# Two PSUM banks reduced by one VectorE instruction in an attention kernel, with a new order of the banks

## The chip, the cores and the metric

The kernel runs on one core of a Trainium2 chip. A core has a matrix engine (TensorE, PE in the profile, with its weight loads shown apart as PEld), a vector engine (VectorE, DVE), a scalar engine (ScalarE, ACT), GpSimd (POOL) and a queue engine that here only issues transfers (SyncE, SP). They run side by side and wait for one another through semaphores. TensorE writes its results to PSUM, a memory of eight banks; one bank holds 128 rows of 512 fp32 numbers. The metric is the time of one execution on the device, in microseconds; lower is better. An execution with the profiler on gives the trace.

## The reference

The function mixes two causal or full attention layers over the same `x` (2,048 rows of 512), each with 32 heads of 16 dimensions:

```python
x = A_x
g = _sigmoid((x * gate_w).sum(-1, keepdims=True))
a = _A_ref(x, A_wqkv, A_wo)
b = _B_ref(x, B_wq, B_wk, B_wv, B_wo, B_beta)
return g * a + (1 - g) * b
```

`_A_ref` is plain softmax attention of every row over all 2,048 rows:

```python
scores = jnp.einsum("bhqd,bhkd->bhqk", q, k) * scale
p = _softmax(scores, axis=-1)
o = jnp.einsum("bhqk,bhkd->bhqd", p, v)
```

`_B_ref` cuts the rows into 4 segments of 512. Within a segment it is causal softmax attention; a memory matrix carried from segment to segment adds a second part, and a gate by head mixes the two. A softmax subtracts the maximum of each row of scores, and it is these row maxima that the change is about.

## The kernel before

**Units, slots, bursts.** The attention is cut into units `(side, g, c)`: side A or B, a group `g` of four heads, and a block `c` of 512 query rows. There are 32 units of each side. A unit of side A has 64 slots, one for each 128 keys and each head; a unit of side B, which is causal and local, has 10. That makes 2,368 slots (`nS`), which the main loop (L1001 and after) walks in order `n`. In each slot `score_part(n)` issues the score product of 128 keys by 512 queries into one of three `st` banks (L726), and ScalarE turns it into exponentials (L749). After every third slot, a burst (`BURST = 3`), TensorE also gets the products of older exponentials with the values, into the one bank `ops` (L783). How many pieces of 128 columns it takes is set by `most()`, so bursts differ. Instead of value products a burst can hold three products of an output projection (L895) or of a later projection (L666).

**Maxima.** Scores are built with keys as rows, so the maximum of a query's scores must be known before its unit starts. It comes from a second set of products with queries as rows: `max_part(m, bank)` issues, for slot `m = n + LEAD` (96 slots ahead), one product of 128 queries by 512 keys (`max_product`, L205) into a PSUM bank, and VectorE reduces that bank to one maximum for each row (L226). For side B, where the mask matters, a slot holds one or two products of different widths in one bank, and VectorE takes each one's maximum under the causal mask by `tensor_tensor_reduce` (L238 in the profile, a custom instruction and a read of its accumulator). The first of the two is issued at once; the second waits in `rows_left` until after the next reduction. When a unit's last maximum is in, `finish_max` combines them (L183), GpSimd splits the result, TensorE transposes it and a transfer puts it into two rows of the unit's queries, so that the score product subtracts the maximum by itself. The list `maxs` fixes which slot has which maximum; those of side B fall on slots with `m % 3 == 0`, the first of a burst.

**The order on TensorE.** It is the order in which the program is written: score, maximum, score, maximum, score, maximum, then the value products of the burst. A score and the maximum product beside it use different halves of the array's rows. TensorE takes its instructions in this order, and one that waits holds those behind it.

**Banks.** Of the eight PSUM banks three are `st`, one is `ops`, and four are the banks of the maxima, made at L606 as four tiles:

```python
banks = [sm_ps.tile([128, CH], F32, name=f"sm{i}") for i in range(4)]
...
max_part(m, lambda: banks[m % 4])
```

So slot `m` uses bank `m % 4`, and its product waits until the reduction of slot `m - 4` is done. The 96 maxima ahead of the main loop (`some_max`) use other tiles, `me_sm`, in the prologue. In the last 96 slots (`wide`), which have no maxima left, the banks serve as further score banks, and at the end they collect the last output products (`close`).

**Waits.** The semaphores are set by the recording layer: it knows which tile an instruction reads or writes and adds a wait where two instructions of different engines touch the same tile.

Of the kernel before, what the change touches and what calls it, by code (L numbers as in the profile page):

```python
# [22 lines left out]
CH = 512  # L23
# [4 lines left out]
SCALE = 0.25  # L28
# [19 lines left out]
def gated_mix(ctx, tc, x, xT, wqkv, a_wo, b_wq, b_wk, b_wv, b_wo, beta, gate_w, out):  # L48
    nc = tc.nc
# [85 lines left out]
    qt, kt_ = {}, {}  # L135
# [33 lines left out]
    def rows(t, h, n):  # L169

        return t[64 * (h // 2):64 * (h // 2) + n, h % 2]
# [19 lines left out]
    def transpose_max(us, pool, tag):  # L191
# [8 lines left out]
        for i, (_, u, ms) in enumerate(us):  # L200
            for r in range(2):
                nc.sync.dma_start(raw(qt[u])[64 * r + 48:64 * r + 50], raw(mt)[32 * i + 16 * r:32 * i + 16 * r + 16])

    def max_product(ps, u, h, s, n0, n, k, k0=0):
        nc.tensor.matmul(ps[:, n0:n0 + n], rows(qt[u][:, :, s * 128:(s + 1) * 128], h, 48), rows(k[:, :, k0:k0 + n], h, 48),  # L205
                         start=True, stop=True)

    rows_left = []

    def flush_rows():  # L210
        while rows_left:
            rows_left.pop(0)()

    def max_part(m, bank):

        u, (r, i) = maxs[m]
        side, g, c = u
        if u not in pmt:
            pmt[u] = mp.tile([128, 4, 4] + [4] * (side == "A"), F32, tag="pm" + side, name="pm")
        pm = pmt[u]  # L220
        ps = bank()
        if side == "A":

            kc, s, h = i // 8, i % 8 // 2, 2 * r + i % 2
            max_product(ps, u, h, s, 0, CH, kt_[u, kc])
            nc.vector.tensor_reduce(pm[:, h, s, kc:kc + 1], ps, axis=AX.X, op=ALU.max)  # L226
            flush_rows()
        else:


            k = kt_[u, c]
            mine = [(2 * r + h, s, 128 * (s == 2) + 256 * (s == 1 and h), 128 * (s + 1))
                    for h, s in (((0, 0), (0, 2)), ((0, 1), (1, 1)), ((1, 0), (1, 2)), ((0, 3),), ((1, 3),))[i]]
            for h, s, n0, w in mine:
                max_product(ps, u, h, s, n0, w, k)
            flush_rows()
            for h, s, n0, w in mine:
                rows_left.append(lambda h=h, s=s, n0=n0, w=w: nc.vector.tensor_tensor_reduce(  # L238
                    out=tri["rest"][:, 0:w], in0=ps[:, n0:n0 + w], in1=tri["mask"][:, CH - w:], scale=-1.0, scalar=3.0e38,
                    op0=ALU.add, op1=ALU.min, accum_out=pm[:, h, s:s + 1]))  # L240
# [464 lines left out]
    def from_bank(n):  # L705

        return nc.vector.tensor_copy if n > wide.start + 4 else nc.scalar.copy
# [3 lines left out]
    def score_part(n):  # L711

        u, j = slots[n]
        side, g, c = u
        q = qt[u]

        if j % 4 == 0:
            pt_[u, j // 4] = pp.tile([128, 4, CH], F32, tag="p", name="p")
            order_p[u, j // 4] = len(order_p)
            assert not queue or order_p[queue[0][1], queue[0][2] // 4] > len(order_p) - 1 - NP  # L720
        p = pt_[u, j // 4]
        h = (0, 2, 1, 3)[j % 4]

        def score(ps, h, b, k, n0, q0):

            nc.tensor.matmul(ps[:, n0:n0 + CH - q0], rows(k[:, :, b * 128:(b + 1) * 128], h, 50),  # L726
                             rows(q[:, :, q0:], h, 50), start=True, stop=True)

        def diagonal(x):
            nc.gpsimd.affine_select(out=x, in_=x, pattern=[[0, 4], [1, 128]], base=0, channel_multiplier=-1,  # L730
                                    compare_op=ALU.is_ge, fill=0.0)

        ps = banks[1 + n % BURST] if n in wide and n // BURST % 2 else st_ps.tile([128, CH], F32, tag="st", name="st")
        if side == "A":
            score(ps, h, j // 4 % 4, kt_[u, j // 16], 0, 0)
        else:
            k = kt_[u, c]
            if j < 8:
                score(ps, h, j // 4, k, 0, 128 * (j // 4))
                if j >= 4:  # L740
                    score(ps, h, 3, k, 384, 384)
            else:
                for f in range(2):
                    score(ps, 2 * (j - 8) + f, 2, k, 256 * f, 256)
        if side == "B" and j >= 8:
            nc.scalar.activation(p[:, 2 * (j - 8):2 * (j - 8) + 2, 0:256], ps.rearrange("p (h t) -> p h t", h=2), AF.Exp,
                                 scale=SCALE)
        else:
            nc.scalar.activation(p[:, h], ps, AF.Exp, scale=SCALE)  # L749
# [141 lines left out]
    def products(ps, t, b, side, o, start, stop):  # L891

        assert (side, o) in ready
        for i, (x, w) in enumerate(((1, 0), (0, 1), (0, 0))):
            yield lambda i=i, x=x, w=w: nc.tensor.matmul(ps, t[:, b, x], halved[side][:, o, w], start=start and i == 0,  # L895
                                                         stop=stop and i == 2)

    def out_rows(c, b):
        return out[c * CH + b * 128:c * CH + (b + 1) * 128, :]
# [31 lines left out]
    part = {}  # L931

    def keep(ps, c, b):
        part[b] = fr.tile([128, D], F32, tag="part", name="part")
        nc.scalar.copy(part[b], ps)

    def leave(ps, c, b):
        t = fr.tile([128, D], F32, tag="res", name="res", bufs=2)
        from_bank(n)(t, ps)
# [97 lines left out]
    for b in range(4):  # L1037
        close(0, "A", NO - 1, b)
        for _, f in fill[-3:]:
            f()  # L1040
        t = fr.tile([128, D], F32, tag="v" if b % 2 else "res", name="res", bufs=2)
        if b < 3:
            (nc.vector.tensor_copy if b % 2 else nc.scalar.copy)(t, banks[b])
            nc.sync.dma_start(out_rows(last, b), t)
            continue

        for cols, copy, queue in ((slice(0, 256), nc.scalar.copy, nc.scalar), (slice(256, 512), nc.vector.tensor_copy, nc.sync)):
            copy(t[:, cols], banks[b][:, cols])
            queue.dma_start(out_rows(last, b)[:, cols], t[:, cols])


# [33 lines left out]
```

## Time and profile before

| | us |
|---|---|
| median of three runs | 1785.6 (1783.46 to 1789.0) |
| the profiled execution, its own time | 1784.4 |
| its span, first to last instruction | 1782.7 |
| maximum reductions (L226), mean of one | 0.682 |
| exponentials (L749), mean of one | 0.601 |
| score products (L726, side A), mean of one | 0.432 |
| maximum products (L205, side A), mean of one | 0.428 |

The profile has views of one execution: busy time by engine; the chain of work that ended last, followed back from the last instruction; groups of equal instructions with their line, operation, tiles and shapes, their count, busy time, mean time, and the idle time of the engine ahead of them with what ended it; a list of waits; a timeline; and sums over stretches of the span. Times are in us unless ns stands beside them. `x1916` is a count. The mean of one instruction runs from its start to its end and can be longer than the spacing of two that follow each other, since they overlap; the ends of TensorE's products are modelled. The granted clock of TensorE was 1.00 of full speed over the whole main loop.

### The profile page before, as it was taken

To read this page: it belongs to the slowest core of one execution; us is meant where nothing else is said; L and a number is where in the kernel's file an instruction comes from. 1 tells how busy PE (TensorE), PEld (TensorE's weight loads), DVE (VectorE), ACT (ScalarE), POOL (GpSimd) and SP (SyncE) were. 2 spreads that over 40 slices of the span, in tenths; PEclk is the share of its full clock that TensorE was granted. 3 is DMA by queue.
4 is the path that set the end of the run, shared out by engine and by line. 5 is a ranking of instruction groups with operands and counts; after the bars stand their busy time and mean duration, and the time that the engine had idled before them with its cause. 6 is when DMAs were issued, how large, how long until landed. Compare 5 with 4: busy or idle time off the path is not lost.

```text
span 1782.7 us, 40694 instructions
## 1 busy us (share of the span) xinstructions
PE 1773.5 (99%) x14945; PEld 912.4 (51%) x14945; DVE 1574.0 (88%) x3330; ACT 1437.9 (81%) x2754; POOL 640.9 (36%) x748
## 2 busy tenths in 40 slices
PE   9999999999999999999999999999999999999999
PEld 7887776444444444444444444444444444444444
DVE  4235777999999999999999999999999999999930
ACT  5455444888888888888888888888888888888884
POOL 3002222414161416443434343343434253435343
PEclk9999999999999999999999999999999999999999
DMA  7667555445463436544454544454545353544542
GB/s 227 219 226 249 189 195 192 132 103 140 108 169 107 134 116 180 147 136 135 134 134 128 146 127 146 128 146 115 157 106 156 115 142 116 147 119 140 144 161 61
DMA packets 142422, 261.55 MB, mean 147 GB/s; under 512 B 36328, under 2 KB 60680, under 8 KB 141712
## 3 DMA queue, kind: packets, MB, share of 16 engines
q1 hardware_dynamic: 140864, 257.69, 49.6%
q8 instruction: 119, 1.95, 0.5%
q0 software_dynamic: 1216, 1.14, 0.2%
q14 instruction: 79, 0.65, 0.1%
q10 hardware_dynamic: 144, 0.13, 0.0%
HBM read 174.39 MB, written 83.25 MB: 145 GB/s over the span
## 4 chain that ended last, share of the span: by engine, by line
PE 93%; DMA 2%; ACT 2%; DVE 1%; POOL 1%; issue 0%; SPq 0%; POOLq 0%; DVEq 0%; ACTq 0%
PE ops L783 33%; PE st L726 27%; PE sm L205 14%; PE pr L314 9%; PE ops L895 4%; PE ops L666 2%; PE sm L895 2%; DMA raw<-xT 1%; POOL mn L374 1%; PE num L496 1%; DMA qdA<-q 0%; DMA vs<-wqkv 0%; DMA qdB<-q 0%; DVE q L377 0%; ACT full L369 0%
## 5 line engine op out<-in xcount | busy, mean ns | idle before, releaser
L749 ACT ACTIVATE p<-st 128x512 f32<-128x512 f32 x2261 | 1189.4, 601 | 152.5 <-PE sm L205 108.6
L226 DVE TENSOR_REDUCE pm<-sm 128x1 f32<-128x512 f32 x2048 | 1280.8, 682 | 11.8 <-PE sm L205 11.6
L726 PE MATMUL st<-qA,kA 50*128 50x512 f32 x2014 | 663.1, 432 | 0.0
L205 PE MATMUL sm<-kA,qA 48*128 48x512 f32 x2048 | 658.9, 428 | 0.2
L783 PE MATMUL ops<-p,vA 128*17 128x128 f32 (+3 forms) x6432 | 551.9, 442 | 0.0
L726 PEld LDWEIGHTS st<-qA,kA 50*128 50x128 f32 x2014 | 327.5, 185 | 415.6 <-ACT p L749 371.0
L205 PEld LDWEIGHTS sm<-kA,qA 48*128 48x128 f32 x2048 | 330.6, 185 | 15.2 <-issue 6.4
L845 POOL TENSOR_TENSOR rcp<-rec,minus 128x32 f32<-128x32 f32 x43 | 234.2, 5446 | 76.3 <-DMA rec<-dend 71.7
L238 DVE CUSTOM_DVE_ANT_0 rest<-sm,mask 128x128 f32<-128x128 f32 (+3 forms) x512 | 247.3, 483 | 1.8 <-PE sm L205 0.3
L783 PEld LDWEIGHTS ops<-p,vA 128*17 128x17 f32 x6432 | 130.4, 96 | 214.7 <-issue 189.7
L730 POOL TENSOR_SCALAR_AFFINE_SELECT p<-p 128x512 f32<-128x512 f32 x128 | 79.4, 637 | 332.4 <-ACT p L749 327.9
L205 PE MATMUL sm<-kB,qB 48*128 48x128 f32 (+3 forms) x512 | 166.2, 384 | 0.0
L726 PE MATMUL st<-qB,kB 50*128 50x512 f32 (+1 forms) x495 | 109.4, 329 | 0.3 <-ACT mt L199 0.3
L377 DVE TENSOR_TENSOR q<-full,q 128x512 fp32r<-128x512 f32 x56 | 38.9, 694 | 70.2 <-ACT q L370 69.3
L726 PEld LDWEIGHTS st<-qB,kB 50*128 50x128 f32 x495 | 69.9, 186 | 59.3 <-ACT p L749 48.7
L783 PE MATMUL ops<-p,vB 128*17 128x128 f32 (+3 forms) x1504 | 87.5, 350 | 0.0
L205 PEld LDWEIGHTS sm<-kB,qB 48*128 48x128 f32 x512 | 79.9, 184 | 0.0
L187 POOL CAST ms<-nm 128x16 fp32r<-128x16 f32 x32 | 6.7, 208 | 203.1 <-DVE nm L183 201.3
L374 POOL TENSOR_SCALAR mn<-full 128x512 f32<-128x512 f32 x24 | 35.7, 1488 | 102.1 <-ACT full L369 81.7
L369 ACT COPY full<-pr 128x512 f32<-128x512 f32 x56 | 32.6, 582 | 39.3 <-PE pr L314 39.0
L187 POOL CAST ms<-pm 128x16 fp32r<-128x16 f32 x32 | 6.3, 196 | 128.5 <-DVE pm L238 128.4
L861 POOL TENSOR_TENSOR v<-v,inv 128x512 f32<-128x512 f32 x31 | 39.9, 1286 | 25.8 <-DMA inv<-rdA 22.1
(190 smaller groups left out, 1626.1 us busy)
## 6 DMA issues: line engine op xcount, KB each, us to landing
kA<-kdA SPq DMA_DIRECT2D x256, 128.0 KB
vA<-vdA SPq DMA_DIRECT2D x31, 544.0 KB
kA<-kdA SPq DMA_DIRECT2D x256, 64.0 KB
kdA<-q SPq DMA_DIRECT2D x32, 256.0 KB
qdB<-q SPq DMA_DIRECT2D x32, 256.0 KB
qA<-qdA SPq DMA_DIRECT2D x64, 128.0 KB
kdB<-q SPq DMA_DIRECT2D x32, 256.0 KB
qB<-qdB SPq DMA_DIRECT2D x64, 128.0 KB
```

The costliest lines, as they stand in the source:

```text
L205: nc.tensor.matmul(ps[:, n0:n0 + n], rows(qt[u][:, :, s * 128:(s + 1) * 128], h, 48), rows(k[:, :, k0:k0 + n], h, 48), start=True, stop=True)
L226: nc.vector.tensor_reduce(pm[:, h, s, kc:kc + 1], ps, axis=AX.X, op=ALU.max)
L238: rows_left.append(lambda h=h, s=s, n0=n0, w=w: nc.vector.tensor_tensor_reduce(out=tri["rest"][:, 0:w], in0=ps[:, n0:n0 + w], in1=tri["mas ...
L314: nc.tensor.matmul(ps, l(a, k), r(b, k), start=(n == 0), stop=(n == 11))
L374: nc.gpsimd.tensor_scalar_min(ph["mn"], full, 0.0)
L726: nc.tensor.matmul(ps[:, n0:n0 + CH - q0], rows(k[:, :, b * 128:(b + 1) * 128], h, 50), rows(q[:, :, q0:], h, 50), start=True, stop=True)
L730: nc.gpsimd.affine_select(out=x, in_=x, pattern=[[0, 4], [1, 128]], base=0, channel_multiplier=-1, compare_op=ALU.is_ge, fill=0.0)
L749: nc.scalar.activation(p[:, h], ps, AF.Exp, scale=SCALE)
L783: nc.tensor.matmul(ops[32 * h:32 * h + 17, q0:q0 + 128 * w], v[:, 17 * h:17 * h + 17], p[:, h, c0:c0 + 128 * w], start=(i == 0), stop=done ...
L845: eng.tensor_tensor(r, rec, minus, op=ALU.pow)
L861: eng.tensor_mul(k["v"], k["v"], k["inv"])
L895: yield lambda i=i, x=x, w=w: nc.tensor.matmul(ps, t[:, b, x], halved[side][:, o, w], start=start and i == 0, stop=stop and i == 2)
```

## The change

Three things change.

1. The four banks become one tile of four banks, and each bank is a slice of it. Because the layer that sets the waits now sees one tile, every instruction that touches a bank goes through `touch`, which declares it independent of the last 24 instructions of other engines that touched other banks only.
2. The order of the banks by slot becomes 0, 1, 2, 0, 3, 2. The first slot of a burst always has bank 0. The other two have banks 1 and 2 in one burst and banks 3 and 2 in the next.
3. In the main loop, where the second and third slot of a burst belong to the same unit of side A, the second one's reduction isn't issued; after the third's product one `tensor_reduce` reads both banks, which lie side by side, and writes two maxima. Where a burst's third slot begins another unit, both are reduced one by one as before. The masked maxima of a slot of side B are all issued at once.

The order of the instructions on TensorE, ScalarE, GpSimd and the transfer queues stays as it was; VectorE has 747 instructions fewer.

```diff
+    def touch(inst, *ps):
+
+        mine = {bank_of[id(p)] for p in ps if id(p) in bank_of}
+        if mine:
+            for e, theirs in touched[-24:]:
+                if not mine & theirs and e.ins.engine != inst.ins.engine:
+                    tc.declare_no_dep(inst.ins, e.ins, reason="another bank of the tile")
+            touched.append((inst, mine))
...
-    def max_part(m, bank):
+    def max_part(m, bank, two=None):
...
-            nc.vector.tensor_reduce(pm[:, h, s, kc:kc + 1], ps, axis=AX.X, op=ALU.max)
-            flush_rows()
+            to = 16 * h + 4 * s + kc
+            if two is not None and m % 3 == 1 and maxs[m + 1:m + 2] and maxs[m + 1][0] == u:
+                half[m] = to, ps
+            elif m - 1 in half:
+
+                (to, ps), (above, other) = sorted(((to, ps), half.pop(m - 1)), key=lambda e: e[0])
+                lo, hi = bank_of[id(ps)], bank_of[id(other)]
+                assert lo < hi
+                touch(nc.vector.tensor_reduce(pm.rearrange("p h s k -> p (h s k)")[:, to:above + 1:above - to],
+                                              two[:, lo:hi + 1:hi - lo], axis=AX.X, op=ALU.max), ps, other)
+                flush_rows()
+            else:
+                touch(nc.vector.tensor_reduce(pm[:, h, s, kc:kc + 1], ps, axis=AX.X, op=ALU.max), ps)
+                flush_rows()
...
             rows_left.pop(0)()
+            if two is not None:
+
+                flush_rows()
...
-    banks = [sm_ps.tile([128, CH], F32, name=f"sm{i}") for i in range(4)]
+    four = sm_ps.tile([128, 4, CH], F32, name="sm")
+    banks = [four[:, i] for i in range(4)]
+    bank_of.update((id(b), i) for i, b in enumerate(banks))
...
-            max_part(m, lambda: banks[m % 4])
+            max_part(m, lambda: banks[(0, 1, 2, 0, 3, 2)[m % 6]], four)
```

The products of scores, maxima and outputs, the exponentials and the copies that touch a bank are wrapped in `touch(..., ps)` in the same way.

More of the change, by code (lines that the diff above doesn't have):

```diff
@@ L202, in transpose_max @@
                 nc.sync.dma_start(raw(qt[u])[64 * r + 48:64 * r + 50], raw(mt)[32 * i + 16 * r:32 * i + 16 * r + 16])
+    bank_of = {}
+    touched = []
+    def touch(inst, *ps):
[5 more added lines that the diff above has]
+            touched.append((inst, mine))
     def max_product(ps, u, h, s, n0, n, k, k0=0):
[L205 to L206 removed]
+        touch(nc.tensor.matmul(ps[:, n0:n0 + n], rows(qt[u][:, :, s * 128:(s + 1) * 128], h, 48), rows(k[:, :, k0:k0 + n], h, 48),
+                               start=True, stop=True), ps)
     rows_left = []
@@ L212, in flush_rows @@
             rows_left.pop(0)()
-    def max_part(m, bank):
+    half = {}
+    def max_part(m, bank, two=None):
         u, (r, i) = maxs[m]
@@ L724, in score @@
         def score(ps, h, b, k, n0, q0):
-            nc.tensor.matmul(ps[:, n0:n0 + CH - q0], rows(k[:, :, b * 128:(b + 1) * 128], h, 50),
-                             rows(q[:, :, q0:], h, 50), start=True, stop=True)
+            touch(nc.tensor.matmul(ps[:, n0:n0 + CH - q0], rows(k[:, :, b * 128:(b + 1) * 128], h, 50),
+                                   rows(q[:, :, q0:], h, 50), start=True, stop=True), ps)
         def diagonal(x):
@@ L894, in products @@
         for i, (x, w) in enumerate(((1, 0), (0, 1), (0, 0))):
-            yield lambda i=i, x=x, w=w: nc.tensor.matmul(ps, t[:, b, x], halved[side][:, o, w], start=start and i == 0,
-                                                         stop=stop and i == 2)
+            yield lambda i=i, x=x, w=w: touch(nc.tensor.matmul(ps, t[:, b, x], halved[side][:, o, w], start=start and i == 0,
+                                                               stop=stop and i == 2), ps)
     def out_rows(c, b):
@@ L934, in keep @@
         part[b] = fr.tile([128, D], F32, tag="part", name="part")
-        nc.scalar.copy(part[b], ps)
+        touch(nc.scalar.copy(part[b], ps), ps)
     def leave(ps, c, b):
         t = fr.tile([128, D], F32, tag="res", name="res", bufs=2)
-        from_bank(n)(t, ps)
+        touch(from_bank(n)(t, ps), ps)
         if b in part:
@@ L1042, in gated_mix @@
         if b < 3:
-            (nc.vector.tensor_copy if b % 2 else nc.scalar.copy)(t, banks[b])
+            touch((nc.vector.tensor_copy if b % 2 else nc.scalar.copy)(t, banks[b]), banks[b])
             nc.sync.dma_start(out_rows(last, b), t)
@@ L1047, in gated_mix @@
         for cols, copy, queue in ((slice(0, 256), nc.scalar.copy, nc.scalar), (slice(256, 512), nc.vector.tensor_copy, nc.sync)):
-            copy(t[:, cols], banks[b][:, cols])
+            touch(copy(t[:, cols], banks[b][:, cols]), banks[b])
             queue.dma_start(out_rows(last, b)[:, cols], t[:, cols])
```

10 lines of the change are left out of this document (5 added, 5 removed).

## The prediction

> **What bounds the kernel now.** I read the busy line, the chain that ended last and the costliest groups first.
>
> ```profile
> span 1782.7 us, 40694 instructions
> ...
> PE 1773.5 (99%) x14945; PEld 912.4 (51%) x14945; DVE 1574.0 (88%) x3330; ACT 1437.9 (81%) x2754; POOL 640.9 (36%) x748
> ...
> PE 93%; DMA 2%; ACT 2%; DVE 1%; POOL 1%; issue 0%; SPq 0%; POOLq 0%; DVEq 0%; ACTq 0%
> ...
> L226 DVE TENSOR_REDUCE pm<-sm 128x1 f32<-128x512 f32 x2048 | 1280.8, 682 | 11.8 <-PE sm L205 11.6
> ```
>
> TensorE carries the chain. The page averages a prologue with the main loop, so next come the loop alone, as a window (columns: PE, PEld, DVE, ACT, POOL busy) and as groups, and the first score and last maximum product, which give its ends.
>
> ```profile
> 336.00:1706.00 1370.00, 1369.94 (x12832) 631.38 (x12831) 1368.02 (x2937) 1211.46 (x2346) 541.43 (x625) 1.00 0.48 133
> ```
> ```profile
> L226 DVE TENSOR_REDUCE pm<-sm 128x1 f32<-128x512 f32 x1916 | 1198.2, 682 | 0.2
> L238 DVE CUSTOM_DVE_ANT_0 rest<-sm,mask 128x512 f32<-128x512 f32 x124 | 84.8, 684 | 0.0
> ...
> L238 DVE CUSTOM_DVE_ANT_0 rest<-sm,mask 128x128 f32<-128x128 f32 x124 | 35.5, 286 | 1.7 <-PE sm L205 0.3
> L183 DVE TENSOR_REDUCE nm<-pm 128x16 f32<-128x64 f32 x29 | 6.0, 206 | 0.0
> ```
> ```profile
> L726 PE MATMUL st<-qA,kA x1977: 386/397/507, 306.7 to 1708.3; 50*128 50x512 f32 x198
> ```
> ```profile
> L205 PE MATMUL sm<-kA,qA x1956: 386/398/506, 300.4 to 1706.0; 48*128 48x512 f32 x196
> ```
>
> In the loop VectorE is as full as TensorE: 1368 of 1370 us. The loop lasts 306.7 to about 1706.3, 1400 us, and holds 2,272 slots with a maximum, 757 bursts of three: 1.849 us each. Which engine sets the pace is seen burst by burst, in the chain of waits (start, duration, what); each st row shown starts a burst.
>
> ```profile
> 917.31 0.43 PE st L726
> ...
> 918.99 0.43 PE st L726
> ...
> 920.67 0.43 PE st L726
> ...
> 922.57 0.43 PE st L726
> ...
> 924.47 0.42 PE st L726
> ```
>
> Bursts take 1.68, 1.68, 1.90, 1.90 us: they differ by TensorE's work on the values (L783), while three reductions would take the same 1.8 each time. So TensorE sets each burst, and VectorE, nearly full, keeps up because four banks, each released alone, let it lag through a short burst and recover in a long one.
>
> **The change, part by part.** (1) *Two reductions become one.* The built program has 747 two-bank reductions, one in nearly every burst. Back to back, one-bank reductions start 0.60 us apart: in the row of 1705.49 below three last 1.88, so (1.88 - 0.68) / 2. A 512-wide masked maximum lasts 684 ns and a 128-wide one 286, 1.04 ns an element; from 64 to 512 the plain reduction gives (682 - 206) / 448 = 1.06. A reduction over 1,024 therefore ends 0.68 + 0.54 = 1.22 us after its start, and frees VectorE 0.60 + 0.54 = 1.14 after. It saves 0.06 a pair, 747 x 0.06 = 45 us of VectorE time. Bounds for its length: 1.21 with the lower slope, 1.36 if it were two whole ones.
>
> The Trainium skill (Perfetto Trace Analysis, Optimizing Scalar/DVE Operations) gives VectorE about 125 ns of fixed cost per PSUM access and advises grouping where the engine is saturated. By it the saving would be 747 x 0.125 = 93 us; the spacing here says 45. The same section says that an engine that is not saturated but leaves bubbles on others may do better with its instructions broken up.
>
> (2) *What the pair makes wait.* Banks now go 0, 1, 2, 0, 3, 2. Bank 2 is the third bank of every burst, and it is released only at the end of the pair of the burst just before; bank 0 is free early, banks 1 and 3 wait for nothing. In the built program the third maximum product waits for just that pair, where before it waited for a single reduction four products back. Behind it in TensorE's queue stand the burst's value products, then the next burst's scores and first maximum product; for those wait ScalarE's exponentials and VectorE's next single reduction. How long release and refill take, by the timelines (start, duration):
>
> ```profile
> 985.41 0.09 DVE L238 DVE_READ_ACCUMULATOR2_ANT pm<- 128x1 f32 x1
> ...
> 985.55 0.19 PEld L205 LDWEIGHTS sm<-kA,qA 48*128 48x128 f32 x2 [0.33 <-DVE pm L238]
> ```
> ```profile
> 1662.57 2.01 DVE L226 TENSOR_REDUCE pm<-sm 128x1 f32<-128x512 f32 x3
> ...
> 1663.32 0.73 PE L205 MATMUL sm<-kA,qA 48*128 48x512 f32 x2
> ```
> ```profile
> 182.14 0.73 PE L205 MATMUL sm<-kA,qA 48*128 48x512 f32 x4
> ...
> 182.68 0.69 DVE L226 TENSOR_REDUCE pm<-sm 128x1 f32<-128x512 f32 x1 [2.00 <-PE sm L205]
> ```
> ```profile
> 1705.49 1.88 DVE L226 TENSOR_REDUCE pm<-sm 128x1 f32<-128x512 f32 x3
> ```
>
> VectorE's end at 985.50 to the weight load: 0.05. A first product with its weights not yet loaded, to the reduction that waits for it: 0.57 (three reductions last 2.01 instead of 1.88, so the third starts at 1662.57 + 2.01 - 0.69 = 1663.89), or 0.54 in the prologue; I take 0.57, the row from the loop. Now TensorE's own part:
>
> ```profile
> 918.92 0.29 PEld L205 LDWEIGHTS sm<-kA,qA 48*128 48x128 f32 x2
> ...
> 919.40 0.18 PEld L205 LDWEIGHTS sm<-kA,qA 48*128 48x128 f32 x1
> ...
> 920.60 0.29 PEld L205 LDWEIGHTS sm<-kA,qA 48*128 48x128 f32 x2
> ...
> 921.09 0.18 PEld L205 LDWEIGHTS sm<-kA,qA 48*128 48x128 f32 x1
> ```
> ```profile
> 922.51 0.50 PE L205 MATMUL sm<-kA,qA 48*128 48x512 f32 x1
> ```
>
> From a burst's first maximum product to its third's weight load 0.48; from there to the next burst's first 1.20 in a short burst and 1.42 in a long one.
>
> Two loops follow. *Pair to pair:* refill 0.57, pair 1.22, release 0.05: 1.84 a burst, whatever TensorE could do. *Over two bursts:* third product of burst k, the rest of k (1.20 or 1.42), first product to reduction 0.57, reduction 0.60, pair 1.22, release 0.05, third product of k+2: 2.44 besides the rest, so 3.64 from a short and 3.86 from a long burst, against 3.58 for long + short and 3.36 for two shorts today. VectorE is idle at some points of both loops, so its 45 us are no gain; with the four separate banks it hid exactly these latencies.
>
> The size: at 1.849 a burst the mean rest is 1.849 - 0.48 = 1.37, and the mean of the two alternating paths (1.37 + 2.44) / 2 = 1.905, or +0.056: +42 us over 757 bursts, a floor. The path takes the worse alternation. Short, short, long, long as above become 1.90 + 3.86 + 1.84 = 7.60 for 7.16, +0.11 a burst: +83 if all were so. Bursts without value products are all alike (1.84) and stay at the floor; between floor and 83 I take +57.
>
> (3) *Causal row maxima* now always lie in bank 0, and both are taken ahead of the pair rather than one after the next reduction.
>
> ```profile
> 900.32 0.55 DVE L238 CUSTOM_DVE_ANT_0 rest<-sm,mask 128x384 f32<-128x384 f32 x1
> 900.79 0.08 DVE L238 DVE_READ_ACCUMULATOR2_ANT pm<- 128x1 f32 x1
> ...
> 901.40 0.28 DVE L238 CUSTOM_DVE_ANT_0 rest<-sm,mask 128x128 f32<-128x128 f32 x1
> 901.60 0.08 DVE L238 DVE_READ_ACCUMULATOR2_ANT pm<- 128x1 f32 x1
> ```
>
> 0.47 + 0.20 = 0.67 stand where 0.60 stood: +0.07 in some 310 bursts, half of them on the path: +11 us.
>
> (4) *What today's loop loses to VectorE* goes. The chain shows such places where row maxima are dense:
>
> ```profile
> 983.42 0.32 PE st L726
> ...
> 984.88 0.32 PE st L726
> ...
> 987.27 0.37 PE st L726
> ```
> ```profile
> PEld sm L205 <- DVE pm L238: 3.1, 10, 0.3
> ```
>
> The burst of 2.39 us is 0.49 over a long one. Once in each of 30 units (74 slots) that would be 15 us; the waits view names 3.1. I take -11.
>
> (5) *The declarations of independence* issue nothing. They keep a product for one bank from waiting on a reduction of another now that all four are one tile; in the built program each waits for its own bank alone, ScalarE's, GpSimd's and the DMA queue's orders and waits stay, and so do prologue and closing. Without that cover every product would wait for the newest pair.
>
> Sum: 1784.4 (this execution, 1.2 under the median) + 57 + 11 - 11 = 1841.
>
> **The rivals.** *Only the pair-to-pair loop decides*, if VectorE picks up the single reduction sooner than 0.57, or the pair ends earlier. Then long bursts keep 1.90 and short ones go from 1.68 to 1.84. The mean of 1.849 allows (1.90 - 1.849) / 0.22 = 23% short ones, 175, if the rest are long; above half are short. With 220: 35 us, less (4)'s 15, +20: 1804. For it: refill at 0.54 in the prologue. Against: 3.86 for two longs exceeds 3.80 by little, but long + short by 0.28.
>
> *The pair costs two whole reductions* (1.36): 0.14 per two bursts, +53 more: 1894. Against: the steady slope.
>
> *Faster:* the third product seldom finds its bank held, since VectorE's load per burst falls to 0.60 + 1.14 = 1.74, under 1.849. It decides where release plus refill fits under the single reduction (0.05 + 0.57 against 0.60) and the single starts straight after the pair. Then TensorE's own bursts remain and (4)'s 15 us come home: 1769. Against: the single cannot start straight away, its product comes 0.57 + 1.20 after the previous third product, and the pair must wait for it. The grouping advice of the Trainium skill quoted above points this way; no row here shows a loop without these waits.
>
> *Nothing happens:* slack in TensorE's bursts that I don't see pays for the waits: 1785. Against: bursts of one kind agree to hundredths.
>
> **How the numbers follow.** Forecast 0.62, pair-to-pair alone 0.18, dear pair 0.05, faster 0.11, nothing 0.04. A measurement here tells about 0.3%, 5 us, from no change. Slower 0.85, same 0.04, faster 0.11. The range reaches below the pair-to-pair case, 1800, and up to +83 and a few for the row maxima, 1870; it leaves out the faster case, no change and the dear pair, 0.20 together.
>
> **What would show it.** In the changed profile: two-bank reductions of 1.21 to 1.23 us; weight loads of maximum products waiting for the two-bank line, hundreds of times, by about 0.1; VectorE no longer full in the loop, idle before single reductions; short bursts at 1.84 or more; loop about 1457 us. Wrong, if VectorE stays full, if those waits are missing, or if long + short still take 3.6.

## The result, and the profile after

| | before | after |
|---|---|---|
| median, us | 1785.6 (five runs, 1783.5 to 1789.0) | 1861.0 (five runs, 1859.1 to 1862.6) |
| the profiled execution, its own time | 1784.4 | 1860.0 |
| its span | 1782.7 | 1858.3 |

The changed kernel takes 1.0422 times as long, with a 95% interval of 1.0407 to 1.0437: 75 us more. The granted clock of TensorE is 1.00 in both main loops.

The page of the changed kernel, busy line, chain by engine and the groups around the maxima. In a group the last columns are busy time, mean ns of one, and idle time ahead with what ended most of it.

```profile
PE 1847.5 (99%) x14945; PEld 997.6 (54%) x14945; DVE 1589.2 (86%) x2583; ACT 1445.1 (78%) x2754; POOL 642.0 (35%) x748
...
PE 93%; DMA 2%; DVE 2%; ACT 1%; POOL 1%; issue 1%; SPq 0%; POOLq 0%; DVEq 0%; ACTq 0%
...
L249 DVE TENSOR_REDUCE pm<-sm 128x2 f32<-128x1024 f32 x747 | 911.2, 1220 | 0.0
...
L253 DVE TENSOR_REDUCE pm<-sm 128x1 f32<-128x512 f32 x554 | 373.5, 688 | 36.6 <-PE sm L217 23.0
L217 PEld LDWEIGHTS sm<-kA,qA 48*128 48x128 f32 x2048 | 335.8, 184 | 62.1 <-DVE pm L249 30.3
```

The pair lasts 1.22 us. VectorE now stands idle ahead of single reductions, until a maximum product has come, and TensorE's weight loads stand idle until a pair ends. That PE is still "99% busy" says little: TensorE's products have modelled ends, and one that waits can show as a longer one (the median of L217 below is 445 ns, for 398 before).

The loop as a window, and the first score and the last maximum product, which give its ends:

```profile
336.00:1706.00 1370.00, 1369.89 (x12144) 680.22 (x12142) 1312.26 (x2083) 1157.62 (x2228) 513.57 (x594) 1.00 0.45 126
```
```profile
L758 PE MATMUL st<-qA,kA x1980: 386/397/504, 307.8 to 1787.8; 50*128 50x512 f32 x198
```
```profile
L217 PE MATMUL sm<-kA,qA x1956: 386/445/502, 301.5 to 1781.6; 48*128 48x512 f32 x196
```

The same 1,370 us hold 688 fewer TensorE instructions (12,144 for 12,832), and VectorE is busy 1312 for 1368. The loop lasts from 307.8 to about 1782, 1474 for 1400: the whole loss lies in it, 1474 / 757 = 1.947 a burst.

The timeline of the changed kernel over two bursts without a causal maximum (start, duration):

```profile
956.16 0.29 PEld L217 LDWEIGHTS sm<-kA,qA 48*128 48x128 f32 x2
...
956.72 0.69 DVE L253 TENSOR_REDUCE pm<-sm 128x1 f32<-128x512 f32 x1 [0.20 <-PE sm L217]
...
957.33 1.22 DVE L249 TENSOR_REDUCE pm<-sm 128x2 f32<-128x1024 f32 x1
...
958.15 0.42 PEld L758 LDWEIGHTS st<-qA,kA 50*128 50x128 f32 x2
...
958.60 0.18 PEld L217 LDWEIGHTS sm<-kA,qA 48*128 48x128 f32 x1
...
959.80 0.29 PEld L217 LDWEIGHTS sm<-kA,qA 48*128 48x128 f32 x2
```

A burst's first product at 956.16; its reduction 0.56 later; the pair 0.61 after that; its end at 958.55; the third product of the next burst at 958.60; the first product of the burst after that at 959.80, 1.20 later. Together 3.64 us for two bursts, the sum that the prediction gave for a path from a short burst. TensorE's products come in the same order in both kernels, so the same two bursts can be found in the trace of before by counting score products. There they start at 922.51 and end at 926.07, 3.56 us, a long one and a short one:

```profile
922.51 0.29 PEld L205 LDWEIGHTS sm<-kA,qA 48*128 48x128 f32 x2
...
926.07 0.29 PEld L205 LDWEIGHTS sm<-kA,qA 48*128 48x128 f32 x2
```

The list of waits has the third product under its releaser:

```profile
PEld sm L217 <- DVE pm L249: 24.3, 92, 0.3
```

Ninety-two waits of 0.26 us are not 75 us, and the wait at 958.60 above isn't among them. The list counts a wait only where the engine shows idle. Here the weight loads of the second and third score (958.15, 0.42) run until 958.57, so of the wait only 0.03 shows as idle time. Matching each third product, by its place in the order, to the pair that frees its bank shows how many there are: of the 680 followed between 400 and 1740 us, the weight loads of 670 start 0.05 us after the pair's end. In the kernel before, a weight load of a maximum product starts so soon after only 65 of 1,809 reductions (400 to 1690 us). In all 670 cases a score's weight load stands just ahead in that way. So nearly every burst is held, and its third product starts on average 0.18 us later behind its first than in the same burst before.

### The profile page after: what moved, and what is told of

It is laid out like the page before. It is cut to its first block, busy times and chain, and to the rows that moved or that the text cites. A ratio compares the mean times of both kernels' runs of the same rounds, so it can differ in the third digit from the quotient of the medians.

```text
span 1858.3 us, 39878 instructions
## 1 busy us (share of the span) xinstructions
PE 1847.5 (99%) x14945; PEld 997.6 (54%) x14945; DVE 1589.2 (86%) x2583; ACT 1445.1 (78%) x2754; POOL 642.0 (35%) x748
## 3 DMA queue, kind: packets, MB, share of 16 engines
q0 software_dynamic: 1216, 1.14, 0.2%
## 4 chain that ended last, share of the span: by engine, by line
PE 93%; DMA 2%; DVE 2%; ACT 1%; POOL 1%; issue 1%; SPq 0%; POOLq 0%; DVEq 0%; ACTq 0%
PE ops L815 32%; PE st L758 25%; PE sm L217 18%; PE pr L344 8%; PE ops L927 4%; PE ops L698 2%; PE sm L927 1%; POOL mn L404 1%; DMA raw<-xT 1%; PE num L526 0%; DMA qdA<-q 0%; DMA vs<-wqkv 0%; DVE q L407 0%; DMA qdB<-q 0%; ACT ex L411 0%
## 5 line engine op out<-in xcount | busy, mean ns | idle before, releaser
L249 DVE TENSOR_REDUCE pm<-sm 128x2 f32<-128x1024 f32 x747 | 911.2, 1220 | 0.0
L217 PE MATMUL sm<-kA,qA 48*128 48x512 f32 x2048 | 737.8, 445 | 0.5 <-DVE pm L249 0.4
L758 PE MATMUL st<-qA,kA 50*128 50x512 f32 x2014 | 652.1, 430 | 0.0
L253 DVE TENSOR_REDUCE pm<-sm 128x1 f32<-128x512 f32 x554 | 373.5, 688 | 36.6 <-PE sm L217 23.0
L217 PEld LDWEIGHTS sm<-kA,qA 48*128 48x128 f32 x2048 | 335.8, 184 | 62.1 <-DVE pm L249 30.3
L217 PE MATMUL sm<-kB,qB 48*128 48x128 f32 (+3 forms) x512 | 166.0, 384 | 0.0
L217 PEld LDWEIGHTS sm<-kB,qB 48*128 48x128 f32 x512 | 79.9, 184 | 0.3 <-DVE pm L253 0.3
```

The source lines that it names most:

```text
L217: touch(nc.tensor.matmul(ps[:, n0:n0 + n], rows(qt[u][:, :, s * 128:(s + 1) * 128], h, 48), rows(k[:, :, k0:k0 + n], h, 48), start=True, s ...
L249: touch(nc.vector.tensor_reduce(pm.rearrange("p h s k -> p (h s k)")[:, to:above + 1:above - to], two[:, lo:hi + 1:hi - lo], axis=AX.X, op ...
L253: touch(nc.vector.tensor_reduce(pm[:, h, s, kc:kc + 1], ps, axis=AX.X, op=ALU.max), ps)
L758: touch(nc.tensor.matmul(ps[:, n0:n0 + CH - q0], rows(k[:, :, b * 128:(b + 1) * 128], h, 50), rows(q[:, :, q0:], h, 50), start=True, stop= ...
```

## The experiments

They are told in three steps: which of the three edits costs the time, how the path is made up, and whether the pair can stand elsewhere.

### Which edit: the pair, the order of the banks, or the one tile

*The new order without pairs.* Every bank is reduced alone, all else as in the changed kernel.

```diff
-            if two is not None and m % 3 == 1 and maxs[m + 1:m + 2] and maxs[m + 1][0] == u:
+            if False and m % 3 == 1 and maxs[m + 1:m + 2] and maxs[m + 1][0] == u:
```

> The new order of the banks and the one tile stay, but every maximum product of side A is reduced by itself. Theory (the pair's late release and the chain first product, single reduction, pair, third product two bursts on): with single releases no product waits for a pair, VectorE is full again. Row maxima still stand back to back, and today two of them take 0.81 us instead of the 0.67 that the prediction took, so VectorE has 0.14 more in some 190 bursts, up to 15 us over the kernel before: 1786 to 1805. Rival (the order of the banks, the single tile or its declarations cost the time): stays at 1850 to 1861.

Measured: 1881.0 us, 1.0539 [1.0521, 1.0557]. The expectation fell, and so did the prediction's view that the pair makes the loss: without any pair the kernel is 20 us slower still. What is left of the change is the order of the banks, the one tile with its declarations, and the moment at which causal maxima are issued. The next two runs part them.

*The kernel before with the new order alone*, four tiles and no declaration:

```diff
-            max_part(m, lambda: banks[m % 4])
+            max_part(m, lambda: banks[(0, 1, 2, 0, 3, 2)[m % 6]])
```

> The kernel before (four tiles of a bank each, a reduction for every bank, its own row maxima, no declaration) with only the order of the banks changed to 0, 1, 2, 0, 3, 2 over six slots. Theory A (the order of the banks is the cause: the third product of a burst must wait for the last maximum of the burst before, since its bank comes back after three products instead of four): a two-burst path of 0.57 + 0.60 + 0.60 + 0.68 + 0.05 = 2.50 plus the rest of a burst (1.20 or 1.42), 3.70 to 3.92 per two bursts against 3.70 before at best; with the row maxima of before, 0.60, it should take some 10 to 20 less than the run with single reductions in the new order (1881), 1855 to 1881, about 1868. Theory B (the single tile, its declarations or the other flush of the row maxima make the loss): the order costs nothing, 1786 to 1800.

Measured: 1876.4, 1.0511 [1.0495, 1.0526]. This one line costs 91 us. Its page and a piece of its timeline:

```profile
L205 PEld LDWEIGHTS sm<-kA,qA 48*128 48x128 f32 x2048 | 330.4, 184 | 81.5 <-DVE pm L226 44.1
```
```profile
957.24 0.29 PEld L205 LDWEIGHTS sm<-kA,qA 48*128 48x128 f32 x2
...
959.75 0.18 PEld L205 LDWEIGHTS sm<-kA,qA 48*128 48x128 f32 x1 [0.17 <-DVE pm L226]
...
960.95 0.29 PEld L205 LDWEIGHTS sm<-kA,qA 48*128 48x128 f32 x2
```

From a first product (957.24) to the third product of the next burst, which waits for a single reduction, 2.51; to the next first product 1.20: 3.71 for two bursts; the same two took 3.36 before. The expectation had 0.57 + 0.60 + 0.60 + 0.68 + 0.05 = 2.50 and 3.70.

*The one tile with its declarations alone*, in the order of before, without pairs and with the causal maxima issued as before:

```diff
-            max_part(m, lambda: banks[(0, 1, 2, 0, 3, 2)[m % 6]], four)
+            max_part(m, lambda: banks[m % 4])
```

> The kernel after with the order of the banks of before (slot modulo 4), a reduction for every bank and the row maxima of before; the one tile of four banks and its declarations stay. Theory A (only the order of the banks costs time): 1783 to 1790, as before, and no weight load that waits for the maximum of the burst before. Theory B (the one tile and its declarations cost time by themselves): clearly slower, 1800 or more.

Measured: 1786.0, 1.0001 [0.9992, 1.0011]; the idle time ahead of its weight loads is the same kind as before.

```profile
L217 PEld LDWEIGHTS sm<-kA,qA 48*128 48x128 f32 x2048 | 330.6, 185 | 15.5 <-issue 7.1
```

So the tile and the declarations cost nothing in the old order, the new order costs 91, and in it the pairs give some 20 back (1881.0 to 1861.0). The causal maxima taken at once weren't run alone: they are what parts the run with the order alone from the run without pairs, 1876.4 and 1881.0, beside the tile, so some 5 us.

### How the path is made up

*A shorter single reduction on the path.* The single reductions of bank 0 read 8 of its 512 columns; the maxima of the other columns are left out.

```diff
-                touch(nc.vector.tensor_reduce(pm[:, h, s, kc:kc + 1], ps, axis=AX.X, op=ALU.max), ps)
+                touch(nc.vector.tensor_reduce(pm[:, h, s, kc:kc + 1], ps[:, 0:8] if two is not None and m % 3 == 0 else ps, axis=AX.X, op=ALU.max), ps)
```

> As the changed kernel, but in the main loop the reduction of a burst's first bank, side A, reads 8 of the 512 columns; the other columns are left out of those maxima. It takes about 0.07 us of VectorE's spacing instead of 0.60. Theory: the two-burst path falls from 2.44 to 1.9 besides the burst's rest and no longer decides; what remains is pair to pair, 1.84 a burst at least, and the row maxima: 1800 to 1825, with the third product still waiting for the pair in most short bursts. Rival 1 (pair to pair alone made the loss): 1850 to 1861. Rival 2 (VectorE's amount of work made it): TensorE alone, about 1770.

Measured: 1840.6, 1.0314 [1.0299, 1.033]: the direction, but 16 less of a gain than the near end of the expectation. The timeline of this run shows why:

```profile
956.27 1.22 DVE L249 TENSOR_REDUCE pm<-sm 128x2 f32<-128x1024 f32 x1
957.49 0.29 DVE L265 CUSTOM_DVE_ANT_0 rest<-sm,mask 128x128 f32<-128x128 f32 x1
...
957.82 0.56 DVE L265 CUSTOM_DVE_ANT_0 rest<-sm,mask 128x384 f32<-128x384 f32 x1
...
958.31 1.22 DVE L249 TENSOR_REDUCE pm<-sm 128x2 f32<-128x1024 f32 x1
...
960.12 1.23 DVE L249 TENSOR_REDUCE pm<-sm 128x2 f32<-128x1024 f32 x1 [0.52 <-PE sm L217]
...
961.93 1.23 DVE L249 TENSOR_REDUCE pm<-sm 128x2 f32<-128x1024 f32 x1 [0.41 <-PE sm L217]
```

The last two pairs, with a shortened single between them, start 1.81 apart; there VectorE waits for TensorE. The two ahead, with causal maxima between them that the edit doesn't touch, start 2.04 apart. Of the 757 bursts 320 have causal maxima in bank 0 (ten for each of the 32 units of side B); the expectation named them, but without a price. Compared burst by burst with the kernel before, by counting score products, the 437 bursts without them lose 43.8 us in the changed kernel and 26.5 here, the 320 with them 30.7 and 28.9.

*A second scratch tile for the causal maxima.* In a slot of side B with two of them both write their masked scores, which nobody reads, into one tile `rest`. Here they write into two.

```diff
-                    out=tri["rest"][:, 0:w], in0=ps[:, n0:n0 + w], in1=tri["mask"][:, CH - w:], scale=-1.0, scalar=3.0e38,
+                    out=tri[f"rest{n0 and 1}"][:, 0:w], in0=ps[:, n0:n0 + w], in1=tri["mask"][:, CH - w:], scale=-1.0, scalar=3.0e38,
...
-    tri["rest"] = dp.tile([128, CH], F32, name="rest")
+    tri["rest0"] = dp.tile([128, CH], F32, name="rest0")
+    tri["rest1"] = dp.tile([128, CH], F32, name="rest1")
```

> As the changed kernel, but the two masked row maxima of a slot of side B write their unused elementwise result to two scratch tiles instead of one. Theory: the second no longer waits for the first's write, two take 0.67 instead of 0.81 us, and since they stand in the chain ahead of the pair in some 190 bursts, 10 to 25 us come back: 1836 to 1850. Rival (row maxima are hidden beside other work): 1857 to 1862.

Measured: 1847.9, 1.0356 [1.034, 1.0371], 13 us less than the changed kernel. Timelines, of the changed kernel first, then of this run:

```profile
971.08 1.22 DVE L249 TENSOR_REDUCE pm<-sm 128x2 f32<-128x1024 f32 x1
972.21 0.41 DVE L265 CUSTOM_DVE_ANT_0 rest<-sm,mask 128x256 f32<-128x256 f32 x1
972.55 0.08 DVE L265 DVE_READ_ACCUMULATOR2_ANT pm<- 128x1 f32 x1
972.67 0.42 DVE L265 CUSTOM_DVE_ANT_0 rest<-sm,mask 128x256 f32<-128x256 f32 x1
...
973.02 1.22 DVE L249 TENSOR_REDUCE pm<-sm 128x2 f32<-128x1024 f32 x1
```
```profile
966.42 0.42 DVE L265 CUSTOM_DVE_ANT_0 rest<-sm,mask 128x256 f32<-128x256 f32 x1
966.76 0.08 DVE L265 DVE_READ_ACCUMULATOR2_ANT pm<- 128x1 f32 x1
966.76 0.42 DVE L265 CUSTOM_DVE_ANT_0 rest<-sm,mask 128x256 f32<-128x256 f32 x1
...
967.11 1.22 DVE L249 TENSOR_REDUCE pm<-sm 128x2 f32<-128x1024 f32 x1
```

With one tile the second causal maximum starts 0.46 after the first, with two 0.34, and the pair 0.81 after the first for 0.69. With one tile the second stands behind a semaphore that VectorE's own instructions raise: it starts 0.04 after the first one's accumulator has been read (972.55 and 0.08 long), while with two it starts together with that read. (It has a wait on this semaphore in both runs; for which count of it, the trace doesn't tell.)

*A shorter pair, every wait and bank kept.* The pair reads 256 of the 512 columns of each of its banks; the maxima of the others are left out.

```diff
-                                              two[:, lo:hi + 1:hi - lo], axis=AX.X, op=ALU.max), ps, other)
+                                              two[:, lo:hi + 1:hi - lo, 0:256], axis=AX.X, op=ALU.max), ps, other)
```

> The kernel after with a pair that reads 256 of the 512 columns of each of its two banks: the maxima of the other columns are left out; every instruction, wait and bank stays. Theory A (a path over two bursts through first product, single, pair, third product and the rest of the burst sets the time): 0.57 + 0.60 + 0.63 + 0.05 = 1.85 plus 1.20 or 1.42, 3.05 to 3.27 over two bursts, under TensorE's own 3.34 to 3.78: the loss goes altogether, 1780 to 1800 (bursts with two row maxima, 0.81 for 0.60, reach 3.48 at most). Theory B (the declarations, the larger number of waits or the pair's queueing cost time whatever its length): above 1820.

Measured: 1781.8, 0.9975 [0.9963, 0.9986]. The order of the banks is the changed kernel's, the number of instructions too, and the loss is gone:

```profile
L253 DVE TENSOR_REDUCE pm<-sm 128x1 f32<-128x512 f32 x554 | 374.2, 689 | 214.9 <-PE sm L217 198.7
L249 DVE TENSOR_REDUCE pm<-sm 128x2 f32<-128x512 f32 x747 | 511.5, 685 | 0.0
...
L217 PEld LDWEIGHTS sm<-kA,qA 48*128 48x128 f32 x2048 | 338.0, 185 | 10.6 <-issue 7.1
```

With a pair of 0.685 VectorE waits 215 us for TensorE. Between 400 and 1690 us a maximum product's weight load starts 0.05 after the pair's end behind 88 of 691 pairs, where the changed kernel has 645 of 654. That is the path as a sum of times: shorten one term by half a microsecond, and the two bursts fit under TensorE's own.

### Whether the pair can stand elsewhere

*Pairs that roll over the slots*, (0, 1), (2, 3), ..., with an order in which a bank comes back after four products; 816 pairs.

```diff
-            if two is not None and m % 3 == 1 and maxs[m + 1:m + 2] and maxs[m + 1][0] == u:
+            if two is not None and m % 2 == 0 and maxs[m + 1:m + 2] and maxs[m + 1][0] == u:
...
-            max_part(m, lambda: banks[(0, 1, 2, 0, 3, 2)[m % 6]], four)
+            max_part(m, lambda: banks[(1, 0, 3, 2)[m % 4]], four)
```

> Two-bank reductions of slots m and m+1 for even m, wherever both are of side A and one unit (816 of them), with the four banks in turn by m % 4, so a bank comes back four slots later as before and no bank comes back each burst. Theory: a pair has the time of one whole burst, 1.85 us, for the 1.84 of refill, pair and release, and no single reduction stands between in most bursts; VectorE's work falls by some 49 us: 1775 to 1805. Rival (a two-bank reduction is too late wherever it is put): 1830 or more.

Measured: 1952.1, 1.0938 [1.0922, 1.0955], the slowest of all; the expectation missed by 150 us. The page and the timeline:

```profile
PE 67%; DVE 27%; issue 2%; DMA 2%; ACT 1%; POOL 1%; SPq 0%; DVEq 0%; POOLq 0%
```
```profile
695.82 0.29 PEld L217 LDWEIGHTS sm<-kA,qA 48*128 48x128 f32 x2
...
696.39 3.49 DVE L249 TENSOR_REDUCE pm<-sm 128x2 f32<-128x1024 f32 x3 [0.36 <-PE sm L217]
...
698.79 0.18 PEld L217 LDWEIGHTS sm<-kA,qA 48*128 48x128 f32 x1 [0.56 <-DVE pm L249]
...
700.21 0.18 PEld L217 LDWEIGHTS sm<-kB,qB 48*128 48x128 f32 x1
```

From the product that the first pair waits for, 695.82: 0.57, one pair 1.14, the next 1.22, 0.05, and the product that the second pair holds starts at 698.79, in the middle of a burst; the next burst begins 1.42 later: 4.39 for two bursts, longer than either path above. VectorE's pairs take 27% of the chain. Two pairs that follow each other let go of four banks in two steps, so four banks are no longer four steps of slack.

*Pairs over the first two banks of every other burst*, 379 of them, banks in the order 3, 2, 1, 0, and the causal maxima moved to a burst's last slot. The line that issued them all at once is gone again.

```diff
-        at_ = [next(m for m in range(len(maxs) + start, len(maxs) + start + 6) if m % 3 == 0)]
+        at_ = [next(m for m in range(len(maxs) + start, len(maxs) + start + 6) if m % 3 == 0) - 1]
...
-            if two is not None and m % 3 == 1 and maxs[m + 1:m + 2] and maxs[m + 1][0] == u:
+            if two is not None and m % 6 == 0 and maxs[m + 1:m + 2] and maxs[m + 1][0] == u:
...
-            if two is not None:
-                flush_rows()
...
-            max_part(m, lambda: banks[(0, 1, 2, 0, 3, 2)[m % 6]], four)
+            max_part(m, lambda: banks[(3, 2, 1, 0)[m % 4]], four)
```

> The pair is kept where a bank still comes back after four products: banks 3, 2, 1, 0 over four slots, the pair over the first two banks of every other burst (379 pairs), all else single, the row maxima of side B taken up at the burst's last slot. Theory A (a pair costs nothing of itself, it was the reuse after three products that cost): the product four slots on from a pair has 2 bursts less two slots to come, VectorE is relieved by 379 x 0.06 = 23 us, and only a short burst after a pair can be held, by at most some 0.16: 1775 to 1800. Theory B (the pair's release is too late wherever it stands, since two banks come free only together after 1.22): 1820 or more, with the weight load of the product four slots on behind the pair in every other burst.

Measured: 1865.3, 1.0446 [1.043, 1.0461]: a miss, and the rival's number. But its chain names another cause beside the pair:

```profile
725.84 1.23 DVE pm L249
727.06 0.46 DVE rest L265
727.59 0.50 PE sm L217 x2
```

The second causal maximum of a slot stood in VectorE's queue behind the pair that followed, and the next product waited for it. So the run doesn't show the pair alone; the next one puts that maximum ahead of the pair.

```diff
             if two is not None and m % 6 == 0 and maxs[m + 1:m + 2] and maxs[m + 1][0] == u:
+                flush_rows()
                 half[m] = to, ps
```

> The run before it (pairs over the first two banks of every other burst, banks 3, 2, 1, 0 over four slots, 379 pairs) with one line more: what is left of the row maxima of side B is queued ahead of the pair, where it stood behind it (pair 1.22, then the second row maximum, then the weight load of the product four slots on). Theory A (its loss of 80 came from that order on VectorE: only bursts around a row maximum were long, 2.3 to 2.5, while the others ran at TensorE's own 1.67 and 1.89): the weight load no longer waits, 1780 to 1795, about as before, since the 23 us that VectorE is relieved of lie beside TensorE. Theory B (the pair's late release itself makes the long bursts): 1830 or more, the long bursts stay.

Measured: 1817.0, 1.0176 [1.0162, 1.019]. Between the two theories: 48 us came from that order on VectorE, 32 stay. The page and the timeline of this run show them at the pair:

```profile
L250 DVE TENSOR_REDUCE pm<-sm 128x2 f32<-128x1024 f32 x379 | 463.4, 1223 | 21.1 <-PE st L756 8.1
L217 PEld LDWEIGHTS sm<-kA,qA 48*128 48x128 f32 x2048 | 324.0, 184 | 44.8 <-DVE pm L250 24.7
```
```profile
672.54 1.22 DVE L250 TENSOR_REDUCE pm<-sm 128x2 f32<-128x1024 f32 x1
...
673.81 0.18 PEld L217 LDWEIGHTS sm<-kA,qA 48*128 48x128 f32 x1 [0.23 <-DVE pm L250]
```

*The same with a shorter pair*, 400 of the 512 columns of each bank; the maxima of the others are left out.

```diff
-                                              two[:, lo:hi + 1:hi - lo], axis=AX.X, op=ALU.max), ps, other)
+                                              two[:, lo:hi + 1:hi - lo, 0:400], axis=AX.X, op=ALU.max), ps, other)
```

> The run before it (1817) with a pair that reads 400 of the 512 columns of each of its two banks: the maxima of the other columns are left out. It asks where the 31 that are left over the kernel before come from. Theory A (the pair joins a slot to the next, so that its first bank comes back three products after the product that the pair waits for: 0.57 + 1.22 + 0.05 = 1.84 against a burst of 1.67 where the burst is short): a pair of about 0.96 ends the path at 1.58, under any burst: 1783 to 1797. Theory B (the pairs' long bursts come from something else in the moved order, such as the other slot of the row maxima): little gain, 1805 to 1817.

Measured: 1786.0, 1.0005 [0.9996, 1.0015]. The 32 us hang on 0.23 us of the pair's length:

```profile
L250 DVE TENSOR_REDUCE pm<-sm 128x2 f32<-128x800 f32 x379 | 375.3, 990 | 39.6 <-PE st L756 30.2
L217 PEld LDWEIGHTS sm<-kA,qA 48*128 48x128 f32 x2048 | 324.9, 185 | 14.9 <-issue 7.1
```

A pair over slots 0 and 1 is late for the bank of slot 0: the product of slot 4 takes that bank, three products, one burst, after the one that the pair waits for. The expectation had 0.57 + 1.22 + 0.05 = 1.84 for this path. In the trace of the run with full pairs, the weight load of the second product lies 0.71 ahead of the pair (median of the 379), so the path takes 1.98, and a short burst 1.67. Compared burst by burst with the kernel before, all of the loop's 30 us are lost in bursts that follow a pair's burst: 19 of them behind the 117 pairs whose burst took 1.60 to 1.75 (0.17 each), 5 behind the 190 whose burst took 1.86 or more (0.03 each). With 400 columns the path is 0.71 + 0.99 + 0.05 = 1.75; the 0.08 that this is over a short burst doesn't show in the time. A pair makes four banks behave like three for its first bank.

No version with full reductions and pairs came under the kernel before. The pair over the first two banks of every burst, and a fifth bank, were not tried.

## Why the prediction was right, and where it was not

It said 1841 in 1800 to 1870 and slower; the median is 1861.0, 75 above before where the sum had 57. The path's terms were taken from the built kernel, in which the order and the pair stand together. So the number holds although the cause was given to the wrong one of the two: on that reading of the cause the run without pairs was expected at 1786 to 1805, and it took 1881.0.

**The pair (1).** Length 1.22, as worked out; at 971.08 a pair in the changed kernel is followed by a causal maximum at 972.21, 1.13 after its start, for which the step had 1.14. That it gives no gain of its own is right only against the kernel before: in the new order each pair takes 0.06 off the path over two bursts (2.44 for 2.50), 0.06 x 757 / 2 = 23 us, and the runs with and without pairs differ by 20. The rule of the Trainium skill that the prediction weighed (Perfetto Trace Analysis, Optimizing Scalar/DVE Operations: about 125 ns of fixed cost per PSUM access) would make it 47; the 0.06 from the spacing is what the runs bear out. The same section's other sentence, that breaking up instructions may help where an engine isn't saturated but holds others, agrees with the pairs over a burst's first two banks, 32 us more with 379 of them than with single reductions and banks reused after four, though VectorE there is nearly full (1332 of 1370 us). It doesn't agree with the pairs of the changed kernel, which took 20 us off.

**What the third product waits for (2).** The mechanism was right: the path over two bursts, its terms (0.57 forecast and 0.56 measured, 0.60 and 0.61, 1.22, 0.05, 1.20) and its sum of 3.64. Its cause was placed wrongly. The step named the pair's late release, and said that the separate banks had hidden these latencies. What had hidden them is the distance at which a bank comes back. In the order 0, 1, 2, 3 the reductions of a burst's three banks are needed 4 products on; the last one, 2.50 after the first product, ends at the first product two bursts later, at least 3.36 away. In the order 0, 1, 2, 0, 3, 2 banks 0 and 2 come back after three, and the burst's last reduction ends at the third product of the very next burst; behind that product stands, in TensorE's queue, the rest of the burst, which is then added to the 2.50. The line with the new order alone costs 91 us, and no run with the old order and single reductions costs any. The pair joined that path and shortened it a little. The prediction did not write out the same path for three single reductions in the new order; that would have shown 2.50 against 2.44 at once.

**The causal maxima (3)** were mis-sized. The step had 0.67 where 0.60 stood, in some 310 bursts, and +11 us. Only 192 of the 320 bursts with causal maxima hold two of them; the others hold one. Two of them back to back take 0.81, because the second waits for the first where both write the same scratch tile. 0.12 of that is worth 13 us by the run with two tiles; by the same price the whole 0.21 is about 23, an estimate.

**What today's loop loses to VectorE (4)**, -11, hardly comes home. With a pair of 0.685, where VectorE waits for TensorE all through the loop, the time is 1781.8, only 3.4 under before. The waits view had named 3.1; the 15 from which the step took 11 came from one burst of 2.39 multiplied by 30 units.

**The declarations (5)** cost nothing, as said: 1786.0 with them and the old order.

Where the 18 us between forecast and result belong stays open, for two counts disagree. By these sizes, 75 measured less 23 for the causal maxima plus at most 4 that come home leaves 52 to 56 for the path, where the step took 57: the miss would lie in (3) and (4). Counted burst by burst against the kernel before, it lies in the path. The 437 bursts without a causal maximum lose 0.100 each and the 320 with one or two 0.096; the 84 that have none in them or in the two bursts on either side lose 0.104, which over all 757 would be 79. The step took 57 / 757 = 0.075, between its floor and the 0.11 of "if all were so", and the upper end was nearer. The causal maxima lengthen the path, but the bursts with two of them took longer before as well (1.92, and 1.81 without any), so little of it shows in the difference. No run leaves the causal maxima out.

**What would show it.** Pair 1.22: yes. Weight loads behind the pair, hundreds of times: yes by their times, 670 of 680, while the list of waits shows 92. VectorE idle ahead of single reductions: 36.6 us for 11.8. Short bursts at 1.84 or more: the chain of waits has

```profile
956.23 0.43 PE st L758
...
958.11 0.43 PE st L758
...
959.87 0.42 PE st L758
...
962.02 0.43 PE st L758
...
963.91 0.26 PE st L758
```

bursts of 1.88, 1.76, 2.15 and 1.89: a short one can be under 1.84 where the next pays, so this mark was too strict. The 164 bursts that took less than 1.75 before take 1.78 in the mean. The loop of 1457 was 1474.

**The rivals.** Pair-to-pair alone (1804) fell for this kernel. Its loop appears where the single is short: there pairs start 1.81 apart, for the 1.84 forecast. The dear pair fell with the 1.22. "Faster" fell with the bank order, not with the pair. What no rival said is that the order by itself could be the whole loss.

## What to carry to other kernels

Where one engine fills a ring of buffers in a fixed order and another empties it, write down for each buffer after how many fills it comes back and how long filling, queueing and emptying take until then; what stands in the queue behind a held fill is added to the path. Merging two emptying instructions gives both buffers back at the end, so the first loses one place of its distance. That cost 32 us where the pair's first bank came back after four products, while the pair took 20 us off where that bank came back after six, as banks 1 and 3 do in the changed kernel. And when several edits come together, work out the path for each edit alone before naming the one that costs.

## What the runs showed that was not expected

- From VectorE's end to the weight load that waits for it: 0.05 us. One row had shown it ahead of the change; it holds behind hundreds of pairs (changed kernel) and of single reductions (the new order alone) alike.
- Two masked maxima that write the same scratch tile stand 0.12 us further apart than two that write different ones (0.46 and 0.34), though nobody reads the tile: the second waits on a semaphore that VectorE itself raises.
- A wait in nearly every burst, 0.18 us on average, can be nearly absent from a list of waits, when another instruction on the same engine fills the time: 92 listed, 670 by the times of the weight loads. The spacing of weight loads (956.16, 958.60, 959.80) showed it where the idle columns did not.
- An engine's busy share fell little (VectorE 1368 to 1312 of 1370 us) while the loop grew by 5%: it was nearly full before the change and after, and it was the order of the banks that decided whether TensorE felt it.
